# One head per product: 64-row and 64-column tiles of the PE array in place of a block-diagonal operand

## The chip, the cores and the metric

The kernel runs on one core of one Trainium2 chip. The metric is the device time of one execution in microseconds. Before the change it was 310.51 us (median of three runs, 310.35 to 310.56). A page of the profile describes one execution; runs at a visibly lower granted TensorE clock over the whole execution are called slow and are left out of comparisons. In the profiles PE is TensorE, PEld its weight loads, DVE the vector engine, ACT the scalar engine. A product's two operands are called its weights, which PEld loads, and its moving columns. L233 is line 233 of the kernel.

## The reference, cut to what matters

```python
def phi(x): return np.where(x > 0, x, np.exp(x) - 1.0) + 1.0
q_p, k_p = phi(q), phi(k)                            # [8, 8, 576, 64]
kv  = np.einsum('bhsd,bhse->bhde', k_p, v)           # per head 64 x 64, sum over 576 tokens
z   = np.sum(k_p, axis=2)
num = np.einsum('bhsd,bhde->bhse', q_p, kv)
den = np.einsum('bhsd,bhd->bhs', q_p, z)[..., None] + 1e-06
x = num / den                                        # then [4608, 512]
h = x @ w_in                                         # 512 -> 2048
g = h * sigmoid(beta * h)
return g @ w_out                                     # 2048 -> 512
```

The two large products (line 333 and line 356 of the kernel before) hold nearly all the arithmetic. The change touches only the small ones: `kv` with its column of sums `z` (65 columns per head), and the numerators with their denominator.

## The kernel before: the parts that matter

A head has 64 dimensions and the PE array 128 rows and columns, so two heads share one product. For kv both heads' k are the weights (128 columns) and both heads' v move (2 x 65 = 130 columns). The 128x130 result holds the wanted blocks on its diagonal and two useless ones beside it; a multiply by a 0/1 mask clears these. The masked operand then serves the numerators of both heads at once.

```python
def kv_mm(b, i, split=False):                 # i: which half of the eight heads
    ...
    for pp in range(2):
        p = 2 * i + pp
        c0 = pp * 2 * (D + 1)
        for j in range(NT):                   # 5 token tiles, accumulated
            nc.tensor.matmul(
                st[b, "kvp"][:, i, c0 : c0 + 2 * (D + 1)],
                st[b, "p"][:, 1, j, p * P : (p + 1) * P],
                vaug[b % 2][:, j, 2 * p : 2 * p + 2, 0 : D + 1],
                start=(j == 0), stop=(j == NT - 1), skip_group_check=True)

def kv_mask(b, i0=0, i1=2):
    nc.vector.tensor_mul(st[b, "kv"][:, i0:i1],
                         st[b, "kvp"][:, i0:i1, 0 : 4 * (D + 1)], kvmask[:, i0:i1])

def num_mm(b, t):                             # t: token tile, 4 of 128 and a tail of 64
    n = rows(t)
    ...
    for p in range(KC):
        c0 = (p % 2) * 2 * (D + 1)
        nc.tensor.matmul(nps[:n, p // 2, c0 : c0 + 2 * (D + 1)],
                         st[b, "qT"][:, t, p, :n],
                         st[b, "kv"][:, p // 2, c0 : c0 + 2 * (D + 1)],
                         start=True, stop=True, skip_group_check=True)
...
for b in range(2, B + 1):                     # n = b + 1: the small products of the next batch
    ...                                       # sit between large ones
        plan[11] = [F(kv_mm, n, 0)]           # slots of the 512 -> 2048 product
        plan[12] = [F(kv_mm, n, 1)]
        plan[13] = [F(kv_mask, n)]
    ...
        for t in range(NT):                   # slots of the 2048 -> 512 product
            plan[1 + 2 * t] = [F(num_mm, n, t)]
            plan[2 + 2 * t] = [F(num_norm, n, t)]
```

I call each such place, small products between two large ones, a **visit**. A steady batch (3 to 7) has seven: two for kv, five for numerators.

Of the kernel before, what the change touches and what calls it, by code (L numbers as in the profile page):

```python
# [10 lines left out]
BF16 = mybir.dt.bfloat16  # L11
# [5 lines left out]
def kernel(  # L17
# [10 lines left out]
    nc = tc.nc  # L28

    B, H, S, D = q.shape  # L30
    DM = H * D
    DFF = moe_w_in.shape[1]
    P = 128
    KC = DM // P
# [4 lines left out]
    NT = NJ + 1  # L39
# [10 lines left out]
    work = ctx.enter_context(tc.tile_pool(name="work", bufs=2))  # L50
# [4 lines left out]
    def att_banks(dtype=F32):  # L55

        n = 512 if dtype == F32 else 1024
        return attps.tile([P, 2, n], dtype, tag="att", name="att")
# [5 lines left out]
    vaug = [consts.tile([P, NT, H, EA], BF16, name=f"vaug{i}") for i in range(2)]  # L64
# [84 lines left out]
    kvmask = consts.tile([P, 2, 4 * (D + 1)], BF16)  # L149
# [35 lines left out]
    st = {}  # L185

    def by_dma(b):
        return b >= DMA_T

    def begin(b):  # L190
        st[b, "p"] = work.tile([P, 2, NT, DM], BF16, tag="qk_p", name="qk_p")
        st[b, "qT"] = work.tile([P, NT, KC, P], BF16, tag="q_pT", name="q_pT")
        st[b, "kv"] = work.tile([P, 2, 4 * (D + 1)], BF16, tag="kv_bd", name="kv_bd")

    def exp_(b, a, h0=0, h1=H):
        if h0 == 0:
# [28 lines left out]
    def kv_mm(b, i, split=False):  # L225

        if i == 0 or split:
            st[b, "kvp"] = att_banks()
        for pp in range(2):
            p = 2 * i + pp  # L230
            c0 = pp * 2 * (D + 1)
            for j in range(NT):
                nc.tensor.matmul(  # L233
                    st[b, "kvp"][:, i, c0 : c0 + 2 * (D + 1)],
                    st[b, "p"][:, 1, j, p * P : (p + 1) * P],
                    vaug[b % 2][:, j, 2 * p : 2 * p + 2, 0 : D + 1],
                    start=(j == 0), stop=(j == NT - 1), skip_group_check=True,
                )

    def kv_mask(b, i0=0, i1=2):  # L240
        nc.vector.tensor_mul(  # L241
            st[b, "kv"][:, i0:i1], st[b, "kvp"][:, i0:i1, 0 : 4 * (D + 1)],
            kvmask[:, i0:i1],
        )

    def rows(t):
        return P if t < NJ else TAIL
# [28 lines left out]
    def num_mm(b, t):  # L276
        n = rows(t)
        nps = att_banks()
        st[b, "n", t] = nps
        for p in range(KC):  # L280
            c0 = (p % 2) * 2 * (D + 1)
            nc.tensor.matmul(  # L282
                nps[:n, p // 2, c0 : c0 + 2 * (D + 1)],
                st[b, "qT"][:, t, p, :n],
                st[b, "kv"][:, p // 2, c0 : c0 + 2 * (D + 1)],
                start=True, stop=True, skip_group_check=True,
            )

    def num_norm(b, t):
        n = rows(t)  # L290
        den = work.tile([P, 2, 4], F32, tag="den", name="den")
        rden = work.tile([P, 2, 4], F32, tag="rden", name="rden")
        xs = work.tile([P, 2, 4, D], BF16, tag="xs", name="xs", bufs=4)
        st[b, "xs", t] = xs
        nv = st[b, "n", t][:n, :, 0 : 4 * (D + 1)].rearrange("p a (h e) -> p a h e", h=4)
        nc.vector.tensor_scalar(den[:n], nv[:, :, :, D], 1e-6, None, ALU.add)  # L296
        nc.vector.reciprocal(rden[:n], den[:n])  # L297
        nc.vector.tensor_mul(  # L298
            xs[:n], nv[:, :, :, 0:D], rden[:n, :, :, None].to_broadcast([n, 2, 4, D])
        )  # L300
        if by_dma(b):
            nc.sync.dma_start_transpose(
                out=x_dst(b, t), in_=xs.rearrange("p a h d -> p (a h d)")[:n]
            )

    def x_dst(b, t):
        if t < NJ:
            return xT[b % 3][:, t]
        return xT_tail[:, :, b * TAIL : (b + 1) * TAIL]
# [96 lines left out]
    def silu_table():  # L406
        nc.scalar.activation(small[:, 1:2], small[:, 0:1], ACTF.Silu)

    begin(0)
    make_beta()  # L410
    st["warm"] = mm_bank([P, 512])
# [8 lines left out]
    v_copy(0, HH, H)  # L420
    warm(1)
    kv_mm(0, 0, split=True)
    kv_mask(0, 0, 1)
    q_trans(0, 2, 3)
    kv_mm(0, 1, split=True)
    kv_mask(0, 1, 2)
    silu_table()
    q_trans(0, 4)
    warm(2)
    num_mm(0, 0)  # L430
    num_norm(0, 0)
    num_mm(0, 1)
    num_norm(0, 1)
    warm(3)
    x_trans(0, 0)
    num_mm(0, 2)
    num_norm(0, 2)
    st["warm"] = mm_bank([P, 512])
    warm(2)
# [3 lines left out]
    def F(f, *a, **k):  # L443
# [10 lines left out]
        5: [F(x_trans, 0, 3)],  # L454
        8: [F(x_trans, 0, 4)],
        17: [F(begin, 1), F(relu, 1, 1)],
        19: [F(relu, 1, 0)],
        21: [F(w_out_scale, 0)],
# [18 lines left out]
        7: [F(v_copy, 1), F(load_next, 3)],  # L477
        9: [F(q_trans, 1, 0, 1, wide=True), F(q_trans, 1, 2, 3, wide=True)],
        10: [F(kv_mm, 1, 0), F(kv_mm, 1, 1), F(kv_mask, 1), F(w_out_scale, 3)],
        11: [F(q_trans, 1, 4, wide=True), F(num_mm, 1, 0), F(num_norm, 1, 0),  # L480
             F(num_mm, 1, 1), F(num_norm, 1, 1)],
# [8 lines left out]
    h_phase(1, xT[1], ALL, {  # L490
        2: [F(x_trans, 1, 4)],
        8: [F(begin, 2), F(relu, 2, 1)],
        10: [F(relu, 2, 0)],
        12: [F(v_copy, 2)],
# [20 lines left out]
    for b in range(2, B + 1):  # L515
        n = b + 1
# [54 lines left out]
```

## Time and profile before

| | before |
|---|---|
| time, median | 310.51 us |
| span of the profiled execution | 308.8 us, granted clock 0.999 |
| PE busy | 289.8 us (94%) |
| kv products | 160 of 130 columns, 57.4 ns from start to start |
| numerators | 160 of 130 columns, 32 of them (tails) as 128x64 tiles |
| mask multiply | 0.70 us per batch, on DVE |

The prediction shows the lines and works out what bounds the kernel.

### The profile page before, as it was taken

To read this page: it belongs to the slowest core of one execution; us is meant where nothing else is said; L and a number is where in the kernel's file an instruction comes from. 1 tells how busy PE (TensorE), PEld (TensorE's weight loads), DVE (VectorE), ACT (ScalarE), POOL (GpSimd) and SP (SyncE) were. 2 spreads that over 40 slices of the span, in tenths; PEclk is the share of its full clock that TensorE was granted. 3 is DMA by queue.
4 is the path that set the end of the run, shared out by engine and by line. 5 is a ranking of instruction groups with operands and counts; after the bars stand their busy time and mean duration, and the time that the engine had idled before them with its cause. 6 is when DMAs were issued, how large, how long until landed. Compare 5 with 4: busy or idle time off the path is not lost.

```text
span 308.8 us, 4264 instructions
## 1 busy us (share of the span) xinstructions
PE 289.8 (94%) x1648; PEld 144.2 (47%) x1669; DVE 138.4 (45%) x263; ACT 169.0 (55%) x212; POOL 48.7 (16%) x67
## 2 busy tenths in 40 slices
PE   4899997799898999999999999999999999999994
PEld 1368444344454454445444544544454444444441
DVE  6863566930666616552754266336633500120021
ACT  3479793268985774287438734782572057107500
POOL 8834255420400320032002000000000000000000
PEclk9999999999999999999999999999999999999999
DMA  8999999999390399639924642404142510010022
GB/s 92 169 207 204 383 270 190 205 241 148 69 189 35 60 161 214 96 71 171 210 76 87 78 136 76 87 17 128 71 85 18 130 68 0 36 68 35 2 68 68
DMA packets 71461, 36.41 MB, mean 118 GB/s; under 512 B 39168, under 2 KB 65808, under 8 KB 71440
## 3 DMA queue, kind: packets, MB, share of 16 engines
q0 software_dynamic: 40880, 20.45, 46.8%
q1 hardware_dynamic: 30560, 15.68, 21.1%
q8 instruction: 13, 0.21, 0.3%
q14 instruction: 8, 0.07, 0.1%
HBM read 36.71 MB, written 9.44 MB: 149 GB/s over the span
## 4 chain that ended last, share of the span: by engine, by line
PE 78%; DVE 8%; ACT 5%; DMA 5%; issue 1%; POOL 1%; ACTq 0%; POOLq 0%
PE mm L333 38%; PE mm L356 32%; DMA q_pT<-qk_p 3%; PE att L282 3%; ACT e L198 3%; DVE qk_p L212 2%; PE att L233 2%; DMA xqk<-in_q_dram 2%; DVE e L211 1%; DVE w_out L179 1%; DVE xs L298 1%; ACT L198 1%; PE mm L316 1%; ACT xT L320 1%; POOL xqk L113 1%
## 5 line engine op out<-in xcount | busy, mean ns | idle before, releaser
L356 PE MATMUL mm<-w_out,g 128*128 128x512 bf16 x557 | 131.3, 379 | 1.4 <-DVE w_out L179 0.2
L339 ACT ACTIVATE g<-mm,beta_c 128x512 bf16<-128x512 f32 (+1 forms) x152 | 98.9, 666 | 58.4 <-PE mm L333 58.2
L333 PE MATMUL mm<-xT,w_in 128*128 128x512 bf16 (+1 forms) x544 | 115.0, 367 | 1.6 <-ACT xT L320 1.6
L333 PEld LDWEIGHTS <-w_in 128*128 128x128 bf16 x608 | 58.5, 98 | 63.8 <-issue 2.1
L356 PEld LDWEIGHTS <-g 128*128 128x128 bf16 x576 | 54.5, 98 | 60.5 <-issue 1.2
L366 DVE COPY y_sb<-mm 128x512 f32<-128x512 f32 x36 | 24.8, 690 | 91.1 <-PE mm L356 89.2
L198 ACT ACTIVATE e<-xqk 128x2560 bf16<-128x2560 bf16 (+1 forms) x18 | 37.1, 2094 | 6.6 <-DVE rbeta L174 3.7
L298 DVE TENSOR_TENSOR xs<-att,rden 128x512 bf16<-128x512 f32 (+1 forms) x40 | 27.6, 689 | 1.6 <-DVE rden L297 0.2
L339 ACT ACT_TABLE_LOAD x4 | 5.1, 1283 | 38.4 <-PE mm L333 38.4
L212 DVE TENSOR_TENSOR qk_p<-r,e 128x2560 bf16<-128x2560 bf16 (+1 forms) x18 | 24.2, 1344 | 0.6
L296 DVE TENSOR_SCALAR den<-att 128x8 f32<-128x8 f32 (+1 forms) x40 | 6.4, 160 | 29.6 <-PE att L282 29.6
L74 POOL DMA_DIRECT2D vraw<-in_v_dram x7 | 6.2, 881 | 82.4 <-DVE vaug L222 78.4
L241 DVE TENSOR_TENSOR kv_bd<-att,kvmask 128x520 bf16<-128x520 f32 (+1 forms) x9 | 5.7, 638 | 28.1 <-PE att L233 28.1
L282 PE MATMUL att<-kv_bd,q_pT 128*128 128x130 bf16 (+1 forms) x160 | 16.0, 222 | 1.6 <-ACT xT L320 0.7
L282 PEld LDWEIGHTS <-q_pT 128*128 128x128 bf16 (+1 forms) x160 | 11.5, 100 | 10.6 <-DVE xs L298 2.7
L205 DVE TENSOR_SCALAR r<-xqk 128x2560 bf16<-128x2560 bf16 (+1 forms) x18 | 13.8, 773 | 5.2 <-DMA xqk<-in_k_dram 2.9
L211 DVE TENSOR_SCALAR e<-e 128x2560 bf16<-128x2560 bf16 (+1 forms) x18 | 13.5, 749 | 4.5 <-ACT e L198 4.5
L333 PE MATMUL mm<-xT_tail,w_in 128*128 128x512 bf16 x63 | 13.9, 379 | 0.1
L233 PE MATMUL att<-vaug,qk_p 128*128 128x130 bf16 x160 | 11.5, 220 | 0.8 <-DVE qk_p L212 0.8
L233 PEld LDWEIGHTS <-qk_p 128*128 128x128 bf16 x160 | 10.2, 97 | 4.0 <-DVE qk_p L212 1.3
L401 PE MATMUL mm<-g,identity 128*128 128x512 bf16 x43 | 11.6, 416 | 0.2 <-issue 0.2
L74 POOL DMA_DIRECT2D xqk<-in_k_dram x7 | 6.4, 908 | 20.7 <-ACT e L198 13.1
(61 smaller groups left out, 115.1 us busy)
## 6 DMA issues: line engine op xcount, KB each, us to landing
out_dram<-y_sb SPq DMA_DIRECT2D x32, 256.0 KB, 2.3
xqk<-in_k_dram POOLq DMA_DIRECT2D x7, 512.0 KB, 11.8
xqk<-in_q_dram POOLq DMA_DIRECT2D x7, 512.0 KB, 11.9
vraw<-in_v_dram POOLq DMA_DIRECT2D x7, 512.0 KB, 10.3
w_in<-in_moe_w_in_dram POOLq DMA_DIRECT2D x4, 512.0 KB, 11.6
g<-in_moe_w_out_dram POOLq DMA_DIRECT2D x2, 1024.0 KB, 16.4
xqk<-in_moe_w_out_dram POOLq DMA_DIRECT2D x1, 1024.0 KB, 16.2
stage<-in_moe_w_out_dram POOLq DMA_DIRECT2D x1, 1024.0 KB, 16.5
```

What stands on the lines that cost most here:

```text
L74: eng.dma_start(out=dst[:, :, 0:NJ, :].rearrange("p h j d -> p h (j d)"), in_=src[b, :, 0:MAIN, :].rearrange("h (p j) d -> p h (j d)", j=NJ),)
L198: nc.scalar.activation(st[b, "e", a][:, h0:h1], xqk[b % NX][:, a, h0:h1], ACTF.Exp)
L205: nc.vector.tensor_scalar(st[b, "r", a][:, h0:h1], xqk[b % NX][:, a, h0:h1], 0.0, None, ALU.max)
L211: nc.vector.tensor_scalar(e, e, 1.0, None, ALU.min)
L212: nc.vector.tensor_add(st[b, "p"][:, a].rearrange("p j (h d) -> p h j d", h=H)[:, h0:h1], st[b, "r", a][:, h0:h1], e,)
L233: nc.tensor.matmul(st[b, "kvp"][:, i, c0 : c0 + 2 * (D + 1)], st[b, "p"][:, 1, j, p * P : (p + 1) * P], vaug[b % 2][:, j, 2 * p : 2 * p + ...
L282: nc.tensor.matmul(nps[:n, p // 2, c0 : c0 + 2 * (D + 1)], st[b, "qT"][:, t, p, :n], st[b, "kv"][:, p // 2, c0 : c0 + 2 * (D + 1)], start= ...
L298: nc.vector.tensor_mul(xs[:n], nv[:, :, :, 0:D], rden[:n, :, :, None].to_broadcast([n, 2, 4, D]))
L333: nc.tensor.matmul(hp[:, c0:c1], w_in_sb[ff // 4][:, kc, (ff % 4) * P : (ff % 4 + 1) * P], x[:, t0:t1, kc, :] if b < B else x[:, kc, c0:c1 ...
L339: nc.scalar.activation(g[:, ff, c0:c1], hp[:, c0:c1], ACTF.Silu, scale=beta_c[:, ff : ff + 1])
L356: nc.tensor.matmul(yp, g_sb[b % 2][:, ff, t * P : (t + 1) * P], w_out_sb[ff // 4][:, ff % 4, :], start=(ff == 0), stop=(ff == FC - 1),)
L366: nc.vector.tensor_copy(y_sb, yp)
```

## The change

The intent: let each head have its own part of the array. The numerators use two 64x128 tiles (rows x columns of the array: rows 0 to 63 and 64 to 127), the kv products two 128x64 tiles (two halves of the columns). Each product then moves 65 columns, no useless block is computed, and the mask becomes a plain copy of half the size. Two tiles can work at once, so in the best case a pair takes half the time of the 130-column product. Against it stands what I call a **drain**: the time that TensorE loses when the tile shape changes, on entry to a visit and on exit.

```diff
-        st[b, "kv"] = work.tile([P, 2, 4 * (D + 1)], BF16, tag="kv_bd", name="kv_bd")
+        st[b, "kv"] = work.tile([P, KC, D + 1], BF16, tag="kv_bd", name="kv_bd")
 ...  kv_mm
             for j in range(NT):
-                nc.tensor.matmul(
-                    st[b, "kvp"][:, i, c0 : c0 + 2 * (D + 1)],
-                    st[b, "p"][:, 1, j, p * P : (p + 1) * P],
-                    vaug[b % 2][:, j, 2 * p : 2 * p + 2, 0 : D + 1], ...
+                for g in range(2):
+                    c0 = p * P + g * D
+                    nc.tensor.matmul(
+                        st[b, "kvp"][g * D : (g + 1) * D, 0, p * (D + 1) : (p + 1) * (D + 1)],
+                        st[b, "p"][:, 1, j, c0 : c0 + D],
+                        vaug[b % 2][:, j, 2 * p + g, 0 : D + 1], ...
 ...  kv_mask
-        nc.vector.tensor_mul(st[b, "kv"][:, i0:i1], st[b, "kvp"][...], kvmask[:, i0:i1])
+        nc.vector.tensor_copy(st[b, "kv"][:, 2 * i0 : 2 * i1], st[b, "kvp"][:, 0, ...])
 ...  num_mm
         for p in range(KC):
-            nc.tensor.matmul(nps[:n, p // 2, c0 : c0 + 2 * (D + 1)],
-                st[b, "qT"][:, t, p, :n], st[b, "kv"][:, p // 2, c0 : c0 + 2 * (D + 1)], ...
+            for g in range(2):
+                gs = slice(g * D, (g + 1) * D)
+                nc.tensor.matmul(nps[:n, g, p * (D + 1) : (p + 1) * (D + 1)],
+                    st[b, "qT"][gs, t, p, :n], st[b, "kv"][gs, p, :], ...
 ...  num_norm: the output of the last multiply is written in the order of heads
```

More of the change, by code (lines that the diff above doesn't have):

```diff
@@ L230, in kv_mm @@
             p = 2 * i + pp
-            c0 = pp * 2 * (D + 1)
             for j in range(NT):
-                nc.tensor.matmul(
-                    st[b, "kvp"][:, i, c0 : c0 + 2 * (D + 1)],
-                    st[b, "p"][:, 1, j, p * P : (p + 1) * P],
-                    vaug[b % 2][:, j, 2 * p : 2 * p + 2, 0 : D + 1],
-                    start=(j == 0), stop=(j == NT - 1), skip_group_check=True,
-                )
-    def kv_mask(b, i0=0, i1=2):
-        nc.vector.tensor_mul(
-            st[b, "kv"][:, i0:i1], st[b, "kvp"][:, i0:i1, 0 : 4 * (D + 1)],
-            kvmask[:, i0:i1],
+                for g in range(2):
[3 more added lines that the diff above has]
+                        st[b, "p"][:, 1, j, c0 : c0 + D],
+                        vaug[b % 2][:, j, 2 * p + g, 0 : D + 1],
+                        start=(j == 0), stop=(j == NT - 1), skip_group_check=True,
+                    )
+    def kv_mask(b, i0=0, i1=2):
+        nc.vector.tensor_copy(
+            st[b, "kv"][:, 2 * i0 : 2 * i1],
+            st[b, "kvp"][:, 0, 2 * i0 * (D + 1) : 2 * i1 * (D + 1)].rearrange(
+                "p (c e) -> p c e", e=D + 1
+            ),
         )
@@ L280, in num_mm @@
         for p in range(KC):
-            c0 = (p % 2) * 2 * (D + 1)
-            nc.tensor.matmul(
-                nps[:n, p // 2, c0 : c0 + 2 * (D + 1)],
-                st[b, "qT"][:, t, p, :n],
-                st[b, "kv"][:, p // 2, c0 : c0 + 2 * (D + 1)],
-                start=True, stop=True, skip_group_check=True,
-            )
+            for g in range(2):
+                gs = slice(g * D, (g + 1) * D)
+                nc.tensor.matmul(
+                    nps[:n, g, p * (D + 1) : (p + 1) * (D + 1)],
+                    st[b, "qT"][gs, t, p, :n], st[b, "kv"][gs, p, :],
+                    start=True, stop=True, skip_group_check=True,
+                )
     def num_norm(b, t):
@@ L298, in num_norm @@
         nc.vector.tensor_mul(
-            xs[:n], nv[:, :, :, 0:D], rden[:n, :, :, None].to_broadcast([n, 2, 4, D])
+            xs.rearrange("p a h d -> p (a h) d").rearrange("p (c g) d -> p g c d", g=2)[:n],
+            nv[:, :, :, 0:D], rden[:n, :, :, None].to_broadcast([n, 2, 4, D])
         )
```

## The prediction

> **What bounds the kernel now.** I read four views in this order: the page's busy table and slices, the chain that ended last, the groups of instructions, and then the timeline and the single instructions of TensorE around the attention products, because that is where the change acts.
>
> ```profile
> PE 289.8 (94%) x1648; PEld 144.2 (47%) x1669; DVE 138.4 (45%) x263; ACT 169.0 (55%) x212; POOL 48.7 (16%) x67
> ...
> PE   4899997799898999999999999999999999999994
> ...
> PE 78%; DVE 8%; ACT 5%; DMA 5%; issue 1%; POOL 1%; ACTq 0%; POOLq 0%
> ```
>
> TensorE is busy in nearly every slice from the third on, and it is 78% of the chain. DVE and ACT are near half. From about 97 us to the end (batches 3 to 8) the sum of PE busy per stretch is 30.1 of every 30.2 us, so whatever TensorE does longer or shorter there moves the end one for one. Before 97 us the chain also runs through DVE and ACT: batch 0's start, and batch 1 between 48 and 62 us, where PE waits for the normalisation.
>
> The change touches the kv products (line 233) and the numerators (line 282):
>
> ```profile
> L282 PE MATMUL att<-kv_bd,q_pT 128*128 128x130 bf16 (+1 forms) x160 | 16.0, 222 | 1.6 <-ACT xT L320 0.7
> L233 PE MATMUL att<-vaug,qk_p 128*128 128x130 bf16 x160 | 11.5, 220 | 0.8 <-DVE qk_p L212 0.8
> ```
>
> A duration of 220 ns is latency; what counts is the step from one start to the next. In the chain, in order of time, a steady batch shows it:
>
> ```profile
> 138.58 0.57 PE att L233 x10
> 139.15 0.86 PE mm L333 x4
> 140.01 0.58 PE att L233 x10
> ...
> 144.91 0.23 PE att L282 x4
> 145.14 1.73 PE mm L356 x8
> ...
> 152.75 0.35 PE att L282 x4
> ```
>
> Ten kv products take 0.575 us and four numerators 0.23 us: 57.4 ns each for 130 moving columns. 320 of them are 18.4 us, the most that is at stake. The last line is different: the tail tile (64 tokens) also has four products of 130 columns, yet costs 0.35 us. Its weights are 64 columns, so it already runs as a 128x64 tile of the array, between 128x128 neighbours:
>
> ```profile
> 122.51 0.42 PE L282 MATMUL att<-kv_bd,q_pT 128*64 128x130 bf16 x4
> 122.86 1.04 PE L356 MATMUL mm<-w_out,g 128*128 128x512 bf16 x4
> ```
>
> This is the most useful place of the trace, since it prices a change of tile shape. The 512-column product before it starts at 122.200 us; its successor usually starts 216 ns later, here 307 ns: 91 to 93 ns lost on entry. The last tail product starts at 122.710 and the next full one at 122.863 instead of 57 ns later: 96 ns lost on exit. The first product after each change is itself some 10 ns late (24 ns for a 128x64 tile). All eight tail numerators, and the 64x128 tail transposes (99.87 and 100.09 us), show 92 to 97 ns per change. So **a visit in another tile shape costs about 0.20 us**, whatever it holds.
>
> **What the Trainium skill says.** "TensorEngine Tiling (Array Packing)", section Key Properties, says that changing the tiling mode, not just the tile, drains the TensorE, and that different tiles can load weights and multiply in parallel. The drain agrees with the 92 to 97 ns above; parallel tiles no instruction of this trace shows, because every tiled group here uses one tile only. "TensorE: Matmul & The Clock Gate", Part 3, puts concurrent tiles some 4 ns apart, and measured 2.38 times for three column tiles, but at 512 columns, not 65. The same page, section Back-to-back issue gap, puts starts no closer than about 25 ns however few columns there are: 65 columns (about 29 ns) are near it. The section LDWEIGHTS gives columns / 1.2 ns, so 53 ns for 64 columns; the trace disagrees: behind a change of shape two 64-column loads start 28 ns apart (two 128-column loads 11 to 15 ns apart). I use the trace.
>
> **The change part by part.**
>
> *Products.* 160 kv products of 130 columns become 320 of 65 with 64-column weights, alternating between two column tiles; 160 numerators become 320 of 65 with 64-row weights, alternating between two row tiles. A 65-column product streams in about 29 ns: the trace's 64-column tail transposes start 27 to 29 ns apart, weight load included. One after the other, a pair costs 2 x 29.5 = 59 ns against 57.4: 320 pairs cost 0.5 us more. Fully side by side, a pair costs about 30 ns: 320 x 27.4 = 8.8 us saved. Weight loads decide what lies between. For 64-row tiles a load takes about 15 ns, so two per pair fit beside 30 ns of streaming. For 64-column tiles a load takes 28 ns and two take 56 ns, so if loads of the two tiles share one path, a kv pair stays at 56 to 60 ns. I choose 38 ns for a full numerator pair (128 pairs x 19.4 = 2.5 us saved), 50 ns for a tail pair, now 64x64 (32 x 10 = 0.3 us), and 52 ns for a kv pair (160 x 5.4 = 0.9 us). Sum: 3.7 us saved. These are choices, not measurements.
>
> *Changes of shape.* Today only the tail tiles leave 128x128. After it every visit does. Steady batches 3 to 7: two kv visits and four full numerator visits each, so 6 x 5 = 30 new ones. Batch 2: one kv visit (both halves together) and three numerators; the first numerator follows the tail transposes, already 64x128, and pays nothing new: 4. Batch 1: one kv, two numerators. Batch 0: two kv visits, the second going straight on to a 64x128 transpose (half a visit), and three numerator visits: 4.5. Together 41.5. Batch 1's two numerator visits lie where PE waits for DVE anyway, so 39.5 are on the path: 39.5 x 0.20 = **7.9 us added**.
>
> *Mask.* The multiply by the mask (520 columns, 699 ns; half of it, 260 columns, 428 ns) becomes a copy of 260 columns. At the same slope of 1.04 ns per column it takes about 430 ns: 0.27 us less of DVE per batch. Only batch 1's instance (51.59 us, 0.70) is on the chain: 0.3 us saved. The mask's memsets stay. The normalisation reads and writes as many elements in another order, with runs of 64: I expect its 0.69 us unchanged.
>
> Sum: 310.5 + 7.9 - 3.7 - 0.3 = **314.4 us**, rounded to 314.5.
>
> **The rivals.**
>
> 1. *Tiles run fully in parallel, weight loads too.* For it: the skill's array packing, and loads that are short in the trace. Against: 64-column loads of 28 ns and products near the issue floor. It gives 310.5 + 7.9 - 8.8 - 0.3 = 309.3 us: even then the drains eat the whole gain. This is why I give so little to faster.
> 2. *Nothing runs in parallel*, because each pair of load and product issues in order some 29 ns after the last. For it: the tail transposes at 27 to 29 ns per pair of instructions show no quicker issue. It gives 310.5 + 7.9 + 0.5 - 0.3 = 318.6 us, and with 35 ns each some 3.5 us more, 322 us.
> 3. *Rows parallel, columns not.* Numerators save 4.2 us, kv nothing: about 314 us, near my centre by itself.
> 4. *The shorter mask copy or freer DVE shows at the end.* The waits speak against it: from 97 us on PE waits for practically nothing but 0.2 us of a DMA, so a faster DVE has nothing to give.
>
> **Range and chances.** Rivals 1 and 2 nearly bracket the outcome: 309 to 319, with a tail to 322 if small products issue slower than 29 ns. I take 309 to 321. The 2% lines lie at 304.3 and 316.7. Faster would need the drain not to occur between these shapes, against all the examples of the trace: 0.03. Slower needs a mean pair of about 52 ns or more, nearly serial: 0.31. Within 2%: 0.66.
>
> **What would show each step.** The 128x512 product after a numerator or kv visit should start some 95 ns late, and so should the visit's first: six more such gaps per steady batch. Numerator pairs: eight starts over 4 x 38 = 150 ns if the row tiles overlap, 236 ns if not. The kv visit of twenty products: 0.52 us if loads bind, 0.30 if the column tiles overlap, 0.59 or more if all is serial. A steady batch (30.2 us now) should take about 30.8 us. The mask group should read about 430 ns. It would be wrong if the changes of shape cost more or less with two tiles in flight, if tiles in different row groups wait for one another's drain, or if the 65-column runs, half of them starting at odd multiples of 65, write or read at a lower rate.

## The result, and the profile after

| | before | after |
|---|---|---|
| time, median of 4 runs each, same rounds | 310.43 us (310.20 to 310.56) | 310.48 us (310.33 to 311.37) |
| ratio | | 1.0008, 95% interval 0.9988 to 1.0029 |
| the changed kernel again, 6 runs | 310.35 us (11 runs) | 310.74 us, ratio 1.0025 (1.0008 to 1.0043) |

A ratio is the mean time of one kernel's fast runs over that of the other's of the same rounds, so it is not quite the ratio of the medians. The two comparisons give +0.08% and +0.25%, and their intervals reach from -0.12% to +0.43%. I had expected 4 us more. The time lies inside my range, the sum that led to its centre was wrong.

The page of the changed kernel, busy lines and chain; then its groups of kv products, numerators and mask copy (columns: line, engine, operation, output<-inputs, tile of the array, shape, count, busy us, mean ns of one, idle us before):

```profile
PE 289.5 (93%) x1963; PEld 136.5 (44%) x1989; DVE 136.4 (44%) x263; ACT 168.9 (55%) x212; POOL 48.2 (16%) x67
...
PE   4889997799898999999999999999999999999994
...
L234 PE MATMUL att<-vaug,qk_p 128*64 128x65 bf16 x320 | 7.7, 197 | 0.9 <-DVE qk_p L212 0.8
...
L242 DVE CAST kv_bd<-att 128x260 bf16<-128x260 f32 x7 | 3.0, 428 | 25.9 <-PE att L234 25.9
```

There are 315 more records of products (the program has 320 more; some records are missing from a trace), yet PE's busy time is the same. The mask copy takes the 428 ns that I had scaled it to.

The chain of waits of the changed kernel over batch 5's visits (start us, length us, what), to be held against the steady batch that the prediction shows:

```profile
168.81 0.44 PE att L234 x20
169.25 0.97 PE mm L337 x4
170.22 0.44 PE att L234 x20
...
175.08 0.23 PE att L286 x8
175.31 1.83 PE mm L360 x8
```

This view needs care. The kv piece fell from 0.575 to 0.44 us, and the numerator piece seems to cost what it did, 0.23. But the large products after it grew: 0.86 became 0.97 for four, 1.73 became 1.83 for eight, because the chain books the drain at a visit's entry to its own piece and the one at its exit to its neighbour. A visit and its neighbour must be added: kv 1.41 against 1.435, numerators 2.06 against 1.96.

The same from the starts of single products in the trace, medians of batches 4 to 7. "Entry" is the lateness of the visit's first product, "out" the time from its last start to the next large product, and "next" the lateness of the second large one:

```
ns                    entry  first to last  out  next   sum
kv, before  (10)         0        518        57     0    575
kv, after   (20)        93        313       126    11    543    -32, twice per batch
full num, before (4)     0        177        59     0    236
full num, after  (8)    96        111       123    10    340   +104, four per batch
tail num, before (4)    93        201       152    11    457
tail num, after  (8)    93        124       122    10    349   -108, once per batch
```

2 x (-32) + 4 x 104 - 108 = 244 ns per steady batch. The stages say the same: the changed kernel's stretches from one first large product to the next are 0.06 us shorter where kv lies and 0.31 us longer where the numerators lie. Batches 4 to 7 make 1.0 us. Batch 3 would add as much as each of them, but in the profile before, its first numerators came 0.36 us late behind the transposing DMA, and in neither profile of the changed kernel, so its numerator stage reads no longer after the change. Batch 2 adds about 0.2, and batch 1 gives 1.0 back; the second profile of the changed kernel has the span of the one before, 308.8 us:

```
stage (first large product to first large product), us   before   after   after again
512->2048 of batch 0                                       15.47    15.46    15.46
2048->512 of batch 0 (holds all of batch 1's attention)    24.60    23.60    23.63
2048->512 of batch 1 (most of batch 2's)                   20.49    20.76    20.76
2048->512 of batch 2 (numerators of batch 3)               15.58    15.52    15.52
512->2048 of batch 4 (kv of batch 5)                       14.96    14.90    14.90
2048->512 of batch 4 (numerators of batch 5)               15.21    15.52    15.52
```

In batch 1 the chain goes through the kv products, the mask and then the vector engine. In the order before, then changed kernel (second profile), in the chain of waits:

```profile
50.40 1.16 PE att L233 x20
...
51.59 0.70 DVE kv_bd L241
```

```profile
50.38 0.77 PE att L234 x40
...
51.18 0.43 DVE kv_bd L242
```

Here the kv visit holds all forty products and its exit drain lies behind the last result, off the chain: 0.39 us less. The mask gives 0.27. The four rescalings of `w_out` that follow gave about 0.2, but they varied from 1.58 to 2.09 us between profiles with the same code there, so that is no effect of the change that I can show.

In the first profile of the changed kernel batch 4's first numerators waited about 0.7 us longer for the transposing DMA. In the second profile they did not. It showed once more among the other kernels' profiles (the run `e2_serial_kv`). Batch 3's first numerators waited in the same way, by 0.2 to 0.6 us, in five profiles, that of the kernel before among them (its chain of waits):

```profile
104.67 9.85 DMA q_pT<-qk_p
114.52 0.05 issue
114.56 0.41 PE att L282 x4
```

In the run `e7_before_tail128`, which does the same work up to there, it did not wait. So I take these waits for a chance of single executions.

### The profile page after: what moved, and what is told of

The parts are those of the page before. It is cut to its first block, busy times and chain, and to the rows that moved or that the text cites. A ratio compares the mean times of both kernels' runs of the same rounds, so it can differ in the third digit from the quotient of the medians.

```text
span 309.6 us, 4899 instructions
## 1 busy us (share of the span) xinstructions
PE 289.5 (93%) x1963; PEld 136.5 (44%) x1989; DVE 136.4 (44%) x263; ACT 168.9 (55%) x212; POOL 48.2 (16%) x67
## 4 chain that ended last, share of the span: by engine, by line
PE 72%; DMA 13%; DVE 7%; ACT 4%; POOL 3%; issue 1%; POOLq 0%; ACTq 0%
PE mm L337 34%; PE mm L360 33%; DMA stage<-in_moe_w_out_dram 6%; DMA w_in<-in_moe_w_in_dram 4%; DMA q_pT<-qk_p 3%; PE att L286 2%; ACT e L198 2%; DVE qk_p L212 2%; DVE w_out L179 1%; PE att L234 1%; DVE e L211 1%; POOL xqk L113 1%; DVE xs L301 1%; DVE y_sb L370 1%; ACT xT L324 1%
## 5 line engine op out<-in xcount | busy, mean ns | idle before, releaser
L360 PEld LDWEIGHTS <-g 128*128 128x128 bf16 x576 | 53.4, 98 | 61.4 <-issue 0.8
L242 DVE CAST kv_bd<-att 128x260 bf16<-128x260 f32 (+1 forms) x9 | 3.6, 398 | 26.8 <-PE att L234 26.8
L286 PEld LDWEIGHTS <-q_pT 64*128 64x128 bf16 (+1 forms) x320 | 7.5, 97 | 15.9 <-issue 7.9
L286 PE MATMUL att<-kv_bd,q_pT 64*128 64x65 bf16 (+1 forms) x320 | 12.0, 194 | 2.6 <-ACT q_pT L269 1.0
L234 PEld LDWEIGHTS <-qk_p 128*64 128x64 bf16 x320 | 6.3, 111 | 6.3 <-issue 4.9
L300 DVE RECIPROCAL rden<-den 128x8 f32<-128x8 f32 (+1 forms) x40 | 8.1, 202 | 1.4
```

Source lines behind the costliest of these rows:

```text
L286: nc.tensor.matmul(nps[:n, g, p * (D + 1) : (p + 1) * (D + 1)], st[b, "qT"][gs, t, p, :n], st[b, "kv"][gs, p, :], start=True, stop=True, s ...
L360: nc.tensor.matmul(yp, g_sb[b % 2][:, ff, t * P : (t + 1) * P], w_out_sb[ff // 4][:, ff % 4, :], start=(ff == 0), stop=(ff == FC - 1),)
```

## The experiments

The theory after the result: **the two tiles overlap fully, for column tiles too, so streaming gives back about all that the drains take.** The rival: small products are simply cheap, tile or no tile, or the drains are cheaper than they look. All edits are against the changed kernel unless said otherwise.

### 1. The changed kernel again

> The changed kernel once more, unedited, as the yardstick for the others. In its first profile batch 4's first numerators began about 0.7 us late, behind the transposing DMA of q_pT, and that run's time was 311.37 us where the other three were 310.3 to 310.6. Theory A (a chance of that run): the fast runs lie at 310.3 to 310.6 us and the profile has no gap of that size in batch 4; a y stage of batch 3 takes 15.5 us as in the other batches. Theory B (the new order of work makes the DMA late): the gap is there again and the time is near 311.

Measured: 310.74 us (310.52 to 312.03). The 2048->512 stage of batch 3 took 15.53 us, as the other batches' did: theory A by the profile. The times lie above what it said, two of the six over 311.5 us, and that stays unexplained.

### 2. and 3. The loop over the tiles outside

```diff
-            for j in range(NT):
-                for g in range(2):
+            for g in range(2):
+                for j in range(NT):
 ...  and in num_mm (only in e1_serial_both)
-        for p in range(KC):
-            for g in range(2):
+        for g in range(2):
+            for p in range(KC):
```

> The same 640 products, weights and changes of tile shape, but the loop over the two tiles is outside: all products of one tile, then all of the other, so neighbours in the queue share a tile. Theory A (the saving comes from two tiles working side by side): starts go from one per 16 ns back to one per 29 ns, so a kv visit of 20 grows from 0.31 to about 0.59 us and a full numerator visit by about 0.10 us; 16 x 0.27 + 35 x 0.10 = some 8 us, 318 us in all. Theory B (65-column products are quick by themselves, whatever the tile): no change, 310.5 us.

> Only the kv products in serial order of tiles; numerators alternate as in the change. Theory A (column tiles overlap too, weight loads included): 16 visits x 0.27 = about 4.3 us more, 314.8 us. Theory B (column tiles were bound by their weight loads and gained little from alternating): less than 1 us more, about 311 us.

Measured: 312.13 us (ratio to before 1.0053, 1.0037 to 1.0069) and 311.53 us (1.0038, 1.0025 to 1.0051). That is some 1.4 and 0.8 us more than the changed kernel, not 8 and 4, so theory A missed in both, and theory B in the first. The second number is theory B's, but experiment 4 shows that its reason (column tiles gain little from alternating) does not hold. In the timeline of `e1_serial_both` the kv visit became a little longer:

```profile
168.84 0.56 PE L234 MATMUL att<-vaug,qk_p 128*64 128x65 bf16 x20
```

against 0.51 in the changed kernel. From first to last start it is 369 ns, against 313; the numerators take 121 against 111. Taken one tile at a time, nineteen steps should be some 0.6 us. So the edit had not done what I meant: the tiles still overlapped, though five products in a row shared one. The changed kernel's own timeline shows how, in batch 1, where four transposes (line 264, rows 0 to 63) stand in the program ahead of sixteen numerators (line 286) of both row tiles:

```profile
52.46 0.23 PE L264 MATMUL att<-identity,qk_p 64*128 64x64 bf16 x2
52.50 0.20 PE L286 MATMUL att<-kv_bd,q_pT 64*128 64x65 bf16 x1
52.52 0.19 PE L264 MATMUL att<-identity,qk_p 64*128 64x64 bf16 x1
52.54 0.19 PE L286 MATMUL att<-kv_bd,q_pT 64*128 64x65 bf16 x1
52.55 0.19 PE L264 MATMUL att<-identity,qk_p 64*128 64x64 bf16 x1
```

The products start out of the program's order. As I read it, while one tile works off its queue, the next product of the other tile goes ahead. So the order of the loops matters little, and to take the overlap away both heads must use one tile.

### 4. and 5. Both heads in one tile

```diff
 ...  e8_kv_one_tile, kv_mm (two copies of 64 partitions then bring the heads to their rows)
-   st[b, "kvp"][g * D : (g + 1) * D, 0, p * (D + 1) : (p + 1) * (D + 1)],
+   st[b, "kvp"][0:D, g, p * (D + 1) : (p + 1) * (D + 1)],
 ...  e9_num_one_tile, num_mm (a wrong result on purpose)
-                gs = slice(g * D, (g + 1) * D)
+                gs = slice(0, D)
```

> The loop order alone did not take the overlap away: in that run products of the two tiles still started side by side, out of the order of the loops. Here the kv products of both heads use the same column tile (both results in partitions 0 to 63, in two banks), with as many products, weight loads and changes of shape; a second copy of 64 partitions brings the second head to its rows, so the result is right, at about 0.43 us of DVE per batch. Theory A (the saving is two tiles side by side): a kv visit's twenty starts take about 19 x 29.5 = 0.56 us instead of 0.31; 10 steady visits x 0.25, the visits of 40 in batches 1 and 2 twice 0.5, batch 0 0.5, and 0.4 us of DVE in batch 1: 4.4 us more than the change, about 315 us. Theory B (products of 65 columns start every 16 ns in any tile): only the DVE part, 311 us.

> The numerators of both heads use the row tile of partitions 0 to 63 (the second head reads the first head's rows: a wrong result on purpose; the same number, shapes and places of products). Theory A (row tiles side by side): eight starts take about 7 x 29 = 0.20 us instead of 0.11; 36 visits on the path x 0.10 = 3.5 us more, 314 us. Theory B (quick in any tile): no change, 310.6 us.

Measured: 314.99 us (ratio 1.0159, 1.0135 to 1.0183) and 315.20 us (1.0167, 1.0142 to 1.0193), each over 4 us above the changed kernel's 310.7. With kv in one tile some 0.4 us of it is the second copy, which stands in batch 1's chain with 0.42 us. Theory A in both; the numerators cost a little more than expected. The chains of waits show the visits, first with kv in one tile, then with the numerators in one tile:

```profile
170.65 0.75 PE att L234 x20
171.40 0.97 PE mm L338 x4
```

```profile
176.43 0.35 PE att L286 x8
176.78 1.83 PE mm L360 x8
```

The pieces grew from 0.44 to 0.75 and from 0.23 to 0.35 us with the same neighbours. Per product: twenty kv starts take 624 ns instead of 313, so **33 ns each in one tile and 16 in two**; eight numerators 231 instead of 111, again 33 each. A pair in one tile would cost 66 ns, more than the 57.4 of the 130-column product: without the overlap the change would lose even before the drains.

### 6. More visits

```diff
-            plan[11] = [F(kv_mm, n, 0)]
-            plan[12] = [F(kv_mm, n, 1)]
+            plan[9]  = [F(kv_mm, n, 0, pps=(0,))]     # ten products per visit
+            plan[10] = [F(kv_mm, n, 0, pps=(1,))]
+            plan[11] = [F(kv_mm, n, 1, pps=(0,))]
+            plan[12] = [F(kv_mm, n, 1, pps=(1,))]
```

> The changed kernel with the kv products of batches 3 to 7 in four visits of ten instead of two of twenty. The work is the same; only the changes of tile shape grow, by 2 visits x 5 batches = 10. Theory A (each visit costs two drains, about 0.2 us together): 2.0 us more, 312.5 us. Theory B (drains are hidden or shared between visits): under 0.5 us more, 310.5 to 311 us.

Measured: 313.05 us (ratio 1.0090, 1.0071 to 1.0109), 2.3 us above the changed kernel. The stage that holds kv grew from 14.90 to 15.35 us, so by 0.45 us for two more visits: 0.22 each. Theory A; the price of a visit, not of a product, is shown by itself.

### 7. Fewer visits

```diff
-            plan[11] = [F(kv_mm, n, 0)]
-            plan[12] = [F(kv_mm, n, 1)]
+            plan[12] = [F(kv_mm, n, 0), F(kv_mm, n, 1)]
 ...
-            for t in range(NT):
-                plan[1 + 2 * t] = [F(num_mm, n, t)]
-                plan[2 + 2 * t] = [F(num_norm, n, t)]
+            for t in (0, 2, 4):
+                ts = (t, t + 1) if t < NJ else (t,)
+                plan[1 + 2 * t] = [F(num_mm, n, u) for u in ts]
+                plan[2 + 2 * t] = [F(num_norm, n, u) for u in ts]
```

> The changed kernel with fewer and longer visits in batches 3 to 7: all 40 kv products in one place, numerators of token tiles 0 and 1 together, 2 and 3 together, the tail alone: four visits per batch instead of seven. Theory A (drains of 0.2 us per visit eat the gain): 3 x 5 x 0.2 = 3.0 us less, 307.5 us, under both kernels. Theory B (drains cost nothing at the end): no change, or slower by waits for the two PSUM buffers, 310.5 us or more.

Measured: 307.62 us (307.12 to 309.31), ratio to before 0.9922 (0.9896 to 0.9948). Theory A, and a version faster than both kernels. In its chain of waits forty kv products stand in one piece and sixteen numerators in another:

```profile
169.61 0.75 PE att L234 x40
170.36 2.70 PE mm L337 x12
...
174.78 0.36 PE att L286 x16
175.14 3.56 PE mm L360 x16
```

Eight more numerators lengthen the piece from 0.23 to 0.36 us. By single starts, twenty kv products more take 314 ns and eight numerators more 126: **31.5 ns per pair in both**, which is the clean price of a pair.

### 8. The drains taken out of the kernel before

```diff
 ...  num_mm of the kernel before
-        n = rows(t)
+        n = P if by_dma(b) else rows(t)      # batches 3 to 7: the tail with 128 columns of weights
```

> The kernel before with one change: in batches 3 to 7 the tail numerators take all 128 columns of the transposed tile as weights (the upper 64 rows of the result are never read), so they stay in the full-array shape and the two drains of each tail visit go. Theory A (a visit in another shape costs 0.2 us): 5 x 0.2 = 1.0 us less, 309.4 us, with nothing else changed. Theory B (the late starts around the tail come from something else about it): no change, 310.4 us.

Measured: 309.60 us (308.59 to 310.14), ratio 0.9971 (0.9948 to 0.9995). The numerator stage of a batch fell from 15.21 to 14.98 us, so by 0.23, as the visits' table asks (457 - 236 = 221 ns). In its chain the tail looks like any other visit:

```profile
181.68 0.23 PE att L282 x4
181.91 5.18 PE mm L356 x24
```

against 0.35 and 5.29 before. Theory A: the drains of the tail were in the kernel before all along, and one line removes them.

### 9. and 10. Half of the change each

```diff
 ...  e3_kv_only: kv in column tiles, numerators as before; a zeroed block-diagonal tile,
 ...  filled by two copies
+        for g in range(2):
+            gs = slice(g * D, (g + 1) * D)
+            nc.vector.tensor_copy(kv[gs, ..., g], kvp[gs, 0, ...])      # shortened
 ...  e4_num_only: numerators in row tiles, kv as before; its diagonal blocks taken out
 ...  by two such copies
```

> Half of the change: kv products as two 64-column tiles, numerators as before on the full array; two copies of 64 partitions fill the diagonal blocks of a tile zeroed once, in place of the mask. Theory A (each kv visit trades about 0.26 us of streaming for 0.20 us of drains; visits of 40 in batches 1 and 2 gain 0.3 us each): about 1 us under before, 309.5 us. Theory B (drains outweigh the overlap for kv): above 310.5 us.

> The other half: numerators as two 64-row tiles, kv products as before on the full array, its diagonal blocks taken out by two copies of 64 partitions. Theory A (a full numerator visit of four products saves 0.11 us and pays 0.20 us of drains; a tail visit pays no new drain and saves 0.11): 4 x 0.10 - 0.11 = 0.29 us more per batch, times 5, and some 0.3 us in batches 0 and 2: about 312 us. Theory B (numerators gain, kv loses): under 310 us.

Measured: kv alone 309.82 us (ratio 0.9980, 0.9957 to 1.0003); numerators alone 312.98 us (1.0092, 1.0067 to 1.0118). The signs are as expected and so are the steady stages: 14.90 and 15.20 us with kv alone, 14.96 and 15.52 with the numerators alone, each its half of the changed kernel's. So **kv in tiles pays a little, numerators in tiles cost**; the gain with kv alone is read from the stages, since its time is not clear of noise. The numerators alone came out 1 us slower than expected; the excess is in batch 1, where in the profiled execution the granted clock (the column of ones and halves before the DMA share) fell to half for some 7 us:

```profile
54.00:56.00 2.00, 1.08 (x7) 0.32 (x5) 1.87 (x7) 0.00 (x0) 0.78 (x1) 0.99 1.53 195
56.00:58.00 2.00, 1.31 (x13) 0.62 (x11) 1.86 (x6) 0.60 (x1) 0.78 (x2) 0.50 1.64 188
```

All six of its runs have a mean clock of 0.988 to 0.997, where the other half of the change has 0.998 to 1.000. That the clock made the whole of that microsecond is likely but not separated.

### 11. Only what pays

```diff
 ...  on top of e3_kv_only
-            plan[11] = [F(kv_mm, n, 0)]
-            plan[12] = [F(kv_mm, n, 1)]
+            plan[12] = [F(kv_mm, n, 0), F(kv_mm, n, 1)]
-        n = rows(t)
+        n = P if by_dma(b) else rows(t)      # num_mm
```

> A version that takes only what pays: kv products as two column tiles, all 40 of a batch in one visit (batches 3 to 7); numerators on the full array, the tail ones with 128 columns of weights, so no numerator visit changes the shape. From the visits as measured (entry and exit 0.09 + 0.10 us, first product 0.01 late): one kv visit is 0.63 + 0.23 = 0.86 us against 2 x 0.575, 0.29 less; the tail visit 0.24 against 0.46, 0.22 less. Theory A: 5 x 0.51 = 2.6 us, with some 0.2 us from batches 1 and 2, under before: about 307.5 us. Theory B (waits for PSUM or DVE take it back): 309 us or more.

Measured: 307.88 us (307.58 to 309.40), ratio to before 0.9929 (0.9908 to 0.9949). Theory A. Its steady stages are 14.67 and 14.98 us, 0.52 us per batch under before, where the sum from single visits had said 0.51. One kv visit in another shape, none for the numerators:

```profile
168.30 0.75 PE att L232 x40
169.06 2.70 PE mm L338 x12
...
181.32 0.23 PE att L287 x4
181.55 5.18 PE mm L361 x24
```

### 12. The copy done twice

```diff
+        for _ in range(2):
             nc.vector.tensor_copy(st[b, "kv"][...], st[b, "kvp"][...])
```

> The changed kernel with the copy that replaced the mask done twice, so the vector engine has 0.43 us more per batch than the change and 0.16 more than before. Theory A (of the DVE saving only batch 1's copy is on the path): 0.3 to 0.45 us more, 311 us, and the stages from batch 3 on are unchanged to 0.05 us. Theory B (the shorter copy also feeds the later batches): over 1 us more.

Measured: inconclusive. The profiled execution fell in the slow state (383.79 us, clock 0.759), so its stages can't be read. The five fast runs spread from 310.46 to 312.99 us at clocks of 0.992 to 1.000 (ratio to before 1.0051, 1.0023 to 1.0079). Their mean is over 1 us above before, as theory B has it, but the two runs at a clock of 1.000 took 310.46 and 311.23 us, so the clock is mixed into it. How much of the shorter mask reaches the end stays read off batch 1's chain, 0.27 us, and not tested.

## Why the prediction was wrong where it was wrong

- **What bounds the kernel**: right. Five times the change of a steady batch's stages is 2.25 us in experiment 6 and 3.25 us in experiment 7; 2.3 and 3.1 us were measured. The exception is batch 3's first numerators, whose chance waits for a DMA (0.2 to 0.6 us) can hide a change.
- **A visit in another tile shape costs 0.20 us**: right in kind and a tenth low. Measured are 93 to 96 ns on entry, 122 to 129 from the last start to the next large product (so some 93 to 100 on exit, less the 29 ns that I gave a 65-column product) and 10 on the next product. With 31.5 ns per pair taken off the table's sums, 228 ns remain for a kv visit and 214 for a numerator visit; experiment 6 gives 0.22 us per added visit, experiment 8 0.23 per removed one. At 0.22 us my 39.5 visits make 8.7 us, not 7.9. The count as a whole was not tested.
- **The products: this step failed**, at "I choose 38 ns for a full numerator pair, 50 ns for a tail pair, 52 ns for a kv pair". The term "3.7 us saved" was mis-sized: a pair costs 31.5 ns in both. The signs that I had named say the same: 0.31 us for the kv visit's starts, 111 ns for eight numerators. 160 kv pairs save 160 x (57.4 - 31.5) = 4.1 us in place of my 0.9; 128 full numerator pairs save 3.3 in place of 2.5; eight tails save 8 x 0.108 = 0.9 in place of 0.3. Together 8.3 us, not 3.7, less about half a microsecond in batch 1 that nobody waits for (an estimate: its 16 full pairs and its tail). The largest part is kv: I took the weight loads of two column tiles to share one path at 28 ns each. They do not: the loads of the two tiles start 2 to 4 ns apart, and in a visit of forty the products, weights included, start every 16 ns. With these sizes my own sum reads 310.5 + 8.7 - 8.3 - 0.3 + 0.5 = 311.1 us; 310.5 and 310.7 were measured. Rival 1, that the tiles run fully in parallel and the drains eat the gain, was what happened, and its 309.3 us was the better number. That the time fell inside my range is owed to its lower end, which I had taken from this rival, and not to my sum.
- **If nothing ran in parallel**: the price was wrong too, on the low side. I took 29.5 ns per product from the transposes; experiments 4 and 5 show 33. Put together, their excesses, less the second copy, would make some 319 us.
- **The mask**: its 428 ns and batch 1's 0.27 us came as worked out. That batch 1 gained 1.0 us in all I had not seen: kv's 0.39 there is larger than elsewhere because all forty products share one visit and its exit drain falls behind the result that the chain waits for.
- **A steady batch of 30.8 us**: it took 30.42, against 30.17 before, for the same reason as the sum.
- **Loads near the issue floor, odd multiples of 65**: neither showed. Starts came 3 ns apart in different tiles.

## What to carry to other kernels

Price a visit and a product apart: a change of tile shape costs the same 0.2 us for eight products as for forty, so gather small tiled products into few visits, or keep a short visit in the shape of its neighbours, even at the cost of columns that nobody reads. When two effects of opposite sign meet in a sum, size both from a trace or give the unmeasured one its whole range in the centre too: here the measured half was right to a tenth and the chosen half off by a factor of two. And check that an ablation has taken away what it was meant to: reordering a loop did not serialise an engine that looks ahead.

## What the Trainium skill lacked or had wrong

- "TensorE: Matmul & The Clock Gate", Part 3, The mechanism, says that products start and end in strict program order. With tiles they do not: numerators of the second row tile started between transposes that stand ahead of them in the program (52.50 us between 52.46 and 52.52), and kv products with five in a row per tile took 369 ns for twenty starts where one tile alone takes 624.
- The same page, section LDWEIGHTS, gives columns / 1.2 ns, so for 64 columns an estimate of 53 ns. As a spacing of loads that is too long here: forty such loads in two column tiles, each with its product, kept pace with one per 16 ns, in one tile with one per 33 ns, and two in one tile started 28 ns apart behind a drain. (The record of a single load lasts 106 to 114 ns; a spacing is not a length.)
- "TensorEngine Tiling (Array Packing)", section Key Properties, names the drain but no price: some 93 to 100 ns at each change of shape and about 10 ns on the first large product after it, the same for 128x64, 64x128 and 64x64 tiles.
- No page has a time for two tiles at work on products this short: 65 columns cost 33 ns one after the other in one tile and 31.5 ns per pair in two, so the overlap is complete at this size.
- "TensorE: Matmul & The Clock Gate", section HAM oscillation, asks for no idle gap above some 3.4 us. That did not suffice here: in the profile of experiment 7 the granted clock was 0.50 for 3.4 us from 48.9 us on, behind a longest wait of 2.0 us (that run took 309.31 us, the other five 307.1 to 308.3), and in that of the numerators alone for 6.8 us from 55.9 us on, with no wait over 1.6 us in batch 1. Nor does the longest wait decide it: in six profiles, the first of the changed kernel among them, it was 1.9 us at the same place and the clock stayed full. The cause stays open.
